# A planned RWKV and MLP kernel: eighth and later weight tiles behind unit 1's diagonal, and a planner with two DMA queues

## The chip, the core and the metric

One core of a Trainium2 chip runs the whole program. Its engines work from instruction queues of their own, each in its written order: TensorE (PE, matmuls, with a row of its own, PEld, for weight loads), VectorE (DVE), ScalarE (ACT), GpSimd (POOL) and SyncE (SP). Semaphores make one engine wait for another. DMAs are requested from SP's queue and from POOL's. The metric is the device time of one execution in microseconds.

## What is computed

An RWKV-like attention runs over 4 batches, 8 heads, 768 steps and 48 channels; two MLPs follow on its 3072 rows of 384 numbers, with 1536 and 2048 hidden columns.

```python
for t in range(S):
    cur = np.einsum('bhd,bhe->bhde', u[None] * kt, vt)
    y[:, :, t] = np.einsum('bhd,bhde->bhe', rt, state + cur)
    state = wt[:, :, :, None] * state + np.einsum('bhd,bhe->bhde', kt, vt)
...
x = (x @ w_a) * (x @ w_b) @ w_out
h = x @ w_in
out = (np.maximum(h, 0) + alpha * np.minimum(h, 0)) @ w_out2
```

## The kernel before, in words

**The attention** is cut into 12 units of 128 steps for half of the batches (`unit`, line 337). A unit has two chunks of 64 steps; in a chunk the step by step sum becomes a triangular matrix `M` (steps by steps) times `v`, plus the state. Pieces of `M` near the diagonal, of 4, 8 or 16 steps (`SUBS`), are summed on DVE from the natural layout `N` (`natural`: products `e`, sums into `A`). The rest of the triangle comes from matmuls on the transposed layout `Tp` (`T` for unit 1), in levels of 4 to 32 steps: `tree` (DVE, line 521) multiplies the decays in, `level` makes the product `psl` on PE, and ACT copies it into `M` (for unit 1 half of it on DVE). The names in the order of a unit: `psl` (levels), `psk` (transposed keys, copied to `kn` by ACT), `psd` (the state's increase), `St` and `Z` (the state and its copies), and at the end `psx` (the unit's result), which ACT casts into `x` with DVE making its remainder. Units 0 and 1 write their triangles to `m` and `M`, and have tiles of their own.

**The diagonal** (`diag`, line 501) goes from `A` to a small buffer `mb` in HBM and comes back into `M` in eight pieces, `d0` to `d3` for two heads: one write and eight loads from SP's queue, each piece a request.

**The first MLP** (`mlp1`, line 778) takes two units at a time, a block, as a right side of 512 columns: 12 steps of 9 `pa`, 9 `pb` and 9 `acc` matmuls. Every factor stands as a high and a low part, so each product is three matmuls. ACT copies `pa` to `a` and casts `g`, DVE multiplies. The attention of the next block runs beside it. After six blocks the second MLP (`hp`, `hb`, `acd`) runs alone.

**The weights** come as 64-bit floats, 128 x 384 to a tile of 0.39 MB (`load_w`, line 271): POOL requests `raw`, ACT takes it apart in three steps (`ws`, `raw`, `ws`), DVE joins (`ws`), ACT casts the high part (`w`), DVE makes the low one (`w`). The tiles of a step of the first MLP are `a`, `b` and `o`. In the kernel before the first tile is requested when a piece of unit 0's diagonal has landed (a one-element copy `tick` on POOL that reads it, `gate`), six tiles can be under way, and the copy ahead of each later request waits for the tile six before it (`behind`, `WL = 6`).

**The order of all this** is made when the program is built, by a list scheduler (`Tasks.run`, line 94). Each task has an engine, a duration that is assumed, a priority (a due time, lower first) and what it reads and writes. The scheduler runs a clock of its own and lets each engine that is free take the first ready task; the order it finds is the written order of each engine's queue. It knows loads as one stream: `DMA_RATE` of 0.33e6 bytes a microsecond, one after the other, and 2.2 us on top. Between 4.5 and 400 us, until the first `pa`, it puts fills on PE (`warm`, matmuls whose result is not used) where PE would have little to do.

## Time and profile before

| | us |
|---|---|
| Three runs, median | 1005.68 |
| Lowest and highest run | 1001.80, 1007.31 |
| The profiled execution | 1007.24 |
| Its span | 1005.5 |

| engine | busy, us | share of the span |
|---|---|---|
| PE | 977.4 | 97% |
| DVE | 727.9 | 72% |
| ACT | 431.3 | 43% |
| POOL | 86.1 | 9% |

The span is from the first to the last instruction; 1.7 us of the execution lie around it. PE's time holds the fills, and matmuls overlap, so 97% is not 97% of its peak. The shares are means over three stages: a start of some 70 us without MLP, a middle to 600 us with attention and first MLP, and the second MLP. In the middle DVE is nearly full, at the end half empty.

### The profile page before, as it was taken

How to read it: one execution, taken by the hardware profiler on the slowest of the kernel's cores; microseconds unless marked ns; L12 is line 12 of the kernel's file. 1: busy time of each engine (PE TensorE's matmuls, PEld its weight loads, DVE VectorE, ACT ScalarE, POOL GpSimd, SP SyncE). 2: the span in 40 equal slices, each digit the busy share in tenths (PEclk: the TensorE clock that was granted, in tenths of full speed). 3: DMA queues.
4: the chain of work that ended last, by engine and by line, in shares of the span. 5: the costliest groups of instructions: out<-in, count | busy, mean ns of one | idle time of the engine just before them, and what ended most of it. 6: DMA issues, size and time to landing. Idle time of an engine off the chain costs nothing.

```text
span 1005.5 us, 21091 instructions
## 1 busy us (share of the span) xinstructions
PE 977.4 (97%) x8800; PEld 822.2 (82%) x8800; DVE 727.9 (72%) x1215; ACT 431.3 (43%) x931; POOL 86.1 (9%) x173
## 2 busy tenths in 40 slices
PE   6989999999999999999999999999999999999998
PEld 3658777878877788778888888898989898999998
DVE  7889989999989979898925668555554646554643
ACT  0696987544535352534438994121211121211111
POOL 1234220100100010000003331000000000000000
PEclk8999999999999999999999999999999999999999
DMA  8795672414333251415026541010100100000000
GB/s 213 189 262 168 179 199 77 135 43 127 85 96 95 68 159 19 129 38 156 17 60 196 181 157 64 1 32 32 32 32 1 32 32 1 32 1 1 32 1 32
DMA packets 78159, 85.61 MB, mean 85 GB/s; under 512 B 55600, under 2 KB 64944, under 8 KB 76784
## 3 DMA queue, kind: packets, MB, share of 16 engines
q1 hardware_dynamic: 70896, 52.81, 19.8%
q0 software_dynamic: 7168, 31.46, 9.7%
q8 instruction: 69, 1.13, 0.5%
q14 instruction: 26, 0.21, 0.1%
HBM read 73.24 MB, written 11.01 MB: 84 GB/s over the span
## 4 chain that ended last, share of the span: by engine, by line
PE 62%; DVE 22%; ACT 7%; DMA 5%; issue 2%; SPq 0%; POOL 0%; DVEq 0%; ACTq 0%; POOLq 0%
PE acd L767 15%; PE hb L767 15%; PE hp L767 10%; PE pa L767 6%; PE pb L767 6%; PE acc L767 6%; DVE e L258 5%; DVE Tp L258 5%; DVE A L482 4%; DMA Tp<-in_rkw_t_dram 3%; DMA N<-in_rkw_n_dram 2%; PE psl L563 2%; DVE N L258 2%; DVE g L258 2%; DVE a L258 2%
## 5 line engine op out<-in xcount | busy, mean ns | idle before, releaser
L767 PE MATMUL acd<-w,g 128*128 128x384 f32 x864 | 192.6, 335 | 0.0
L949 ACT CAST g<-g 128x512 fp32r<-128x512 f32 x96 | 59.6, 621 | 283.0 <-PE hb L767 173.0
L767 PE MATMUL acc<-g,w 128*128 128x512 f32 x648 | 174.4, 398 | 1.1 <-ACT g L829 1.1
L767 PE MATMUL pa<-x,w 128*128 128x512 f32 x648 | 161.2, 393 | 0.7 <-ACT a L818 0.5
L767 PE MATMUL pb<-x,w 128*128 128x512 f32 x648 | 160.0, 391 | 0.7 <-ACT w L317 0.4
L767 PEld LDWEIGHTS acd<-w,g 128*128 128x128 f32 x864 | 154.2, 188 | 1.8
L767 PEld LDWEIGHTS pa<-x,w 128*128 128x128 f32 x648 | 121.0, 189 | 27.8 <-ACT a L818 1.1
L767 PEld LDWEIGHTS pb<-x,w 128*128 128x128 f32 x648 | 120.9, 188 | 27.0 <-ACT w L317 0.9
L767 PEld LDWEIGHTS acc<-g,w 128*128 128x128 f32 x648 | 118.7, 188 | 26.0 <-ACT g L829 1.7
L258 DVE TENSOR_TENSOR g<-g,g 128x512 fp32r<-128x512 f32 x96 | 66.2, 689 | 81.5 <-ACT g L949 80.9
L258 DVE TENSOR_TENSOR Tp<-Tp 112x1024 f32<-112x1024 f32 (+2 forms) x132 | 106.4, 806 | 12.4 <-DMA Tp<-in_rkw_t_dram 7.8
L767 PE MATMUL hp<-x,w 128*128 128x512 f32 x432 | 102.9, 391 | 0.0
L767 PE MATMUL hb<-x,w 128*128 128x512 f32 x432 | 102.0, 389 | 0.0
L767 PEld LDWEIGHTS hb<-x,w 128*128 128x128 f32 x432 | 81.1, 188 | 16.8
L829 ACT CAST g<-a 128x512 fp32r<-128x512 f32 x72 | 44.5, 618 | 117.1 <-DVE a L258 111.5
L767 PEld LDWEIGHTS hp<-x,w 128*128 128x128 f32 x432 | 80.8, 188 | 16.0
L767 PE MATMUL hb<-w,g 128*128 128x384 f32 x288 | 92.5, 335 | 0.0
L482 DVE TENSOR_REDUCE A<-e 128x16 f32<-128x768 f32 (+15 forms) x148 | 85.6, 578 | 1.6
L940 DVE TENSOR_SCALAR g<-hp,al 128x512 f32<-128x512 f32 x48 | 36.0, 750 | 63.0 <-PE hp L767 63.0
L258 DVE TENSOR_TENSOR a<-a,pb 128x512 f32<-128x512 f32 x72 | 49.0, 681 | 22.2 <-PE pb L767 21.5
L818 ACT COPY a<-pa 128x512 f32<-128x512 f32 x72 | 42.0, 583 | 40.9 <-PE pa L767 40.6
L258 DVE TENSOR_TENSOR g<-a,g 128x512 fp32r<-128x512 f32 x72 | 49.3, 685 | 10.7 <-ACT g L829 10.6
(83 smaller groups left out, 1093.0 us busy)
## 6 DMA issues: line engine op xcount, KB each, us to landing
raw<-in_wt_dram POOLq DMA_DIRECT2D x68, 384.0 KB, 4.0
Tp<-in_rkw_t_dram SPq DMA_DIRECT2D x33, 448.0 KB, 5.5
N<-in_rkw_n_dram SPq DMA_DIRECT2D x10, 1152.0 KB, 7.5
x2d<-x POOLq DMA_DIRECT2D x36, 128.0 KB, 2.1
x2r<-x2d SPq DMA_DIRECT2D x36, 128.0 KB, 2.2
out_dram<-o SPq DMA_DIRECT2D x24, 192.0 KB, 1.9
V<-in_v_s_dram SPq DMA_DIRECT2D x11, 384.0 KB, 6.4
Z<-in_v_s_dram SPq DMA_DIRECT2D x44, 96.0 KB, 3.1
```

What stands on the lines that cost most here:

```text
L258: nc.vector.tensor_tensor(out=out, in0=a, in1=b, op=op)
L482: nc.vector.tensor_reduce(out=v[:, :, d:d + (n - 1) * (SUB + 1) + 1:SUB + 1], in_=part(st["e"], 0, n), axis=AX.X, op=ALU.add)
L563: nc.tensor.matmul(out=st["ps"][o0:o0 + ms, cc, q, zc * i:zc * i + zc], lhsT=t[b0:b0 + 48, 1, q0 + q, t0:t0 + ms], rhs=r[b0:b0 + 48, q0 + ...
L767: nc.tensor.matmul(out=out, lhsT=lhsT, rhs=rhs, start=start, stop=stop)
L818: nc.scalar.copy(c["a", f], c["pa"])
L829: nc.scalar.copy(c["g", f][:, 0], c["a", f])
L940: nc.vector.tensor_scalar(out=st["m", f], in0=st["h", f], scalar1=0.0, scalar2=al[:, f:f + 1], op0=ALU.min, op1=ALU.mult)
L949: nc.scalar.copy(st["g", f][:, 0], st["m", f])
```

## The change

**Requests.** The first seven tiles are requested at once behind unit 0's piece. The eighth waits for a piece of unit 1's diagonal (`M1d2`) by a second one-element copy, and each tile from the eighth on for the tile six before it. To make this possible the generators of the tiles are started in another order (`weights`).

**The planner.** `Queues` takes the place of the single stream: the requests of SP and of POOL stand in two lines, whose heads share a rate by the size of their packets; a transfer's cost has a part per packet; one marked `last` (the diagonal's write) goes only when all requests ahead of it are done. Durations of some tasks are set anew (weight steps on ACT, `psl`, `psk`, `psx`, the MLPs' matmuls, some SP requests). And up to 75 us ACT and DVE don't start a task if one that is more urgent by 4 will be ready within 0.5 us (`soon`).

```diff
+class Queues:
+    def __init__(self):
+        self.rings, self.open, self.n, self.t = {}, set(), 0, 0.0
+    def issue(self, key, ring, now, nbytes, packet, kind):
+        rate = 255e3 if kind == "slow" else 400e3
+        cost = nbytes / packet / 16 * (0.009 + packet * 16 / rate)
+        self.open.add(self.n)
+        self.rings.setdefault(ring, []).append(
+            [key, now + (1.0 if ring == "Pool" else 0.4), cost, self.n, kind, min(max(packet, 256), 6144)])
+        self.n += 1
+    def next(self, until):
+        while until > self.t:
+            heads = [q[0] for q in self.rings.values() if q]
+            act = [x for x in heads if x[1] <= self.t + 1e-9 and not (x[4] == "last" and min(self.open) < x[3])]
...
+            share = sum(x[5] for x in act) / (0.87 if len(act) == 1 and act[0][5] > 300 else 1.0)
+            end = min([self.t + min(x[2] / x[5] for x in act) * share, until] + later)
+            for x in act:
+                x[2] -= (end - self.t) * x[5] / share
...
+                    return end + 1.1, x[0]
...
-    DMA_RATE = 0.33e6
-    DMA_LAT = 2.2
...
+        def soon(eng, p, dur):
+            c, at_ = {}, {}
+            for i, end in ends.items():
+                for s in succ[i]:
+                    if t[s][0] == eng and t[s][2] < p - 4.0:
+                        c[s] = c.get(s, 0) + 1
+                        at_[s] = max(at_.get(s, 0.0), end + (self.LAT[t[i][0]] if t[i][0] != eng else self.SAME.get(eng, 0.0)))
+            return any(c[s] == need[s] and at_[s] < now + min(0.5, dur) for s in c)
...
+                        if now < 75.0 and eng in ("ACT", "DVE") and soon(eng, p, t[i][1]):
+                            break
...
         gate = len(prev) == 1
+        second = len(prev) == 7 + 1
         if gate:
             after = list(after) + ["m1/d2"]
-        if len(prev) > WL:
+        if second:
+            after = list(after) + ["M1d2"]
+        if len(prev) > 7:
             behind = prev[-1 - WL]
...
+            if second:
+                nc.gpsimd.tensor_copy(tick, M[96:97, 1, 0, 0, 32:33])
...
-        add("ACT", act(384), pr, sign, r=[raw], w=[ws, raw + "/h"], alloc=("ws", ws))
-        add("ACT", act(384), pr, expo, r=[raw], w=[raw + "/h"])
-        add("ACT", act(384), pr, low, r=[raw, ws], w=[ws])
+        add("ACT", 0.53, pr, sign, r=[raw], w=[ws, raw + "/h"], alloc=("ws", ws))
+        add("ACT", 0.455, pr, expo, r=[raw], w=[raw + "/h"])
+        add("ACT", 0.53, pr, low, r=[raw, ws], w=[ws])
...
-            add("SP", 0.6, p, out_, r=[an], w=[mbn], nbytes=131072)
+            add("SP", 0.6, p, out_, r=[an], w=[mbn], nbytes=131072, packet=1024, kind="last")
...
-            add("PE", 1.2 + 0.22 * nf, p, mms, r=nm(f"{T}/r", bs) + nm(f"{T}/k", bs), w=[ps],
+            add("PE", (1.15 if h == 32 or z == 32 else 1.6 if h == 16 else 1.8) + 0.22 * nf, p, mms, r=nm(f"{T}/r", bs) + nm(f"{T}/k", bs), w=[ps],
...
-    MM = 0.2155
+    MM = 0.228
...
         weights((load_w((nm, f), wt1[f, i], start[0] + (start[1] - start[0]) / F1 * f - wlead + i)
-                 for f in range(F1) for i, nm in enumerate("abo")), WL - 1)
+                 for f in range(F1) for i, nm in enumerate("abo")), WL - 1, 7, 2)
```

**What moves.** First PE's queue from its start to unit 0's last `psl`; `warm` are the fills, the `psl` rows unit 0's levels of 4, 8, 16 and 32 steps. Before:

```order
L1015 MATMUL warm<-idt 128x512 x9
L563 MATMUL psl<-Tp 60x32 x32
L1015 MATMUL warm<-idt 128x512 x3
L563 MATMUL psl<-Tp 56x32 x32
L1015 MATMUL warm<-idt 128x512 x3
L563 MATMUL psl<-Tp 48x32 x32
L1015 MATMUL warm<-idt 128x512 x4
L563 MATMUL psl<-Tp 32x32 x32
```

Now:

```order
L1082 MATMUL warm<-idt 128x512 x11
L630 MATMUL psl<-Tp 60x32 x32
L1082 MATMUL warm<-idt 128x512 x2
L630 MATMUL psl<-Tp 56x32 x32
L1082 MATMUL warm<-idt 128x512 x3
L630 MATMUL psl<-Tp 48x32 x32
L1082 MATMUL warm<-idt 128x512 x5
L630 MATMUL psl<-Tp 32x32 x32
```

The fills lie otherwise: two more ahead of the first level, one fewer behind it, one more ahead of the last. In the same place on DVE's queue (`a` and `A` are the sums of units 0 and 1, `Tp` is unit 0's tree), before:

```order
L258 TENSOR_TENSOR N<-N 128x4x48
L258 TENSOR_TENSOR Tp<-Tp 112x2x512
L258 TENSOR_TENSOR e<-N 128x4x48
L258 TENSOR_TENSOR Tp<-Tp 112x512
L482 TENSOR_REDUCE a_89<-e 128x4
L258 TENSOR_TENSOR Tp<-Tp 112x2x256x2
L258 TENSOR_TENSOR e<-n_91,un 128x768
L258 TENSOR_TENSOR Tp<-Tp 112x256
L258 TENSOR_TENSOR e<-e,n_90 128x768
L258 TENSOR_TENSOR Tp<-Tp 112x2x128x4
```

Now:

```order
L320 TENSOR_TENSOR N<-N 128x4x48
L320 TENSOR_TENSOR e<-N 128x4x48
L549 TENSOR_REDUCE a_89<-e 128x4
L320 TENSOR_TENSOR Tp<-Tp 112x2x512
L320 TENSOR_TENSOR Tp<-Tp 112x512
L320 TENSOR_TENSOR Tp<-Tp 112x2x256x2
L320 TENSOR_TENSOR Tp<-Tp 112x256
L320 TENSOR_TENSOR e<-n_91,un 128x768
L320 TENSOR_TENSOR e<-e,n_90 128x768
L320 TENSOR_TENSOR Tp<-Tp 112x2x128x4
```

The last product and sum of unit 0's diagonal (`e`, `a`) come ahead of the tree's first steps.

The second place is ACT's queue from unit 1's last copy of `psl` to the second cast of its `x`; `raw`, `ws` and `w` are the weight steps. Before:

```order
L669 COPY St_79<-psd_743 112x384
L302 ACTIVATE ws<-raw 128x384
L308 ACTIVATE raw<-raw 128x384
L302 ACTIVATE ws<-raw 128x384
L296 ACTIVATE ws<-raw 128x384
L317 CAST w<-ws 128x384
L308 ACTIVATE raw<-raw 128x384
L718 CAST x<-psx 128x3x128
L317 CAST w<-ws 128x384
L302 ACTIVATE ws<-raw 128x384
L296 ACTIVATE ws<-raw 128x384
L718 CAST x<-psx 128x3x128
```

Now:

```order
L736 COPY St_79<-psd_744 112x384
L384 CAST w<-ws 128x384 x2
L785 CAST x<-psx 128x3x128
L363 ACTIVATE ws<-raw 128x384
L785 CAST x<-psx 128x3x128
```

Nine weight steps stood between the state's copy `St` and the second cast; now there are three.

The third place is PE's queue where the result of unit 5 (`psx`) stands among the last steps of the second block. Before:

```order
L767 MATMUL pb<-x,w 128x512 x9
L767 MATMUL acc_2456<-g_3260,w 128x512
L767 MATMUL acc_2457<-g_3260,w 128x512
L767 MATMUL acc_2458<-g_3260,w 128x512
L767 MATMUL acc_2456<-g_3260,w 128x512
L767 MATMUL acc_2457<-g_3260,w 128x512
L767 MATMUL acc_2458<-g_3260,w 128x512
L767 MATMUL acc_2456<-g_3260,w 128x512
L767 MATMUL acc_2457<-g_3260,w 128x512
L767 MATMUL acc_2458<-g_3260,w 128x512
L708 MATMUL psx<-M,Z 32x64 x64
```

Now:

```order
L834 MATMUL acc_2390<-g_3214,w 128x512
L834 MATMUL acc_2391<-g_3214,w 128x512
L834 MATMUL acc_2392<-g_3214,w 128x512
L834 MATMUL pa<-x,w 128x512 x9
L775 MATMUL psx<-M,Z 32x64 x64
L834 MATMUL acc_2390<-g_3214,w 128x512
L834 MATMUL acc_2391<-g_3214,w 128x512
L834 MATMUL acc_2392<-g_3214,w 128x512
L834 MATMUL pb<-x,w 128x512 x9
L834 MATMUL acc_2390<-g_3255,w 128x512
```

`psx` stood behind the last `pb` of that block and nine `acc` after it; now it stands ahead of that `pb`, right behind the last `pa`.

## Rows read from the trace of the kernel before

**Rows 1.** By stretch: us, busy PE, PEld, DVE, ACT, POOL (instructions), clock, DMA share, GB/s.

```profile
38.00:70.00 32.00, 28.50 (x626) 17.62 (x626) 28.18 (x60) 30.84 (x67) 10.02 (x18) 1.00 0.87 242
70.00:175.00 105.00, 99.85 (x1187) 80.49 (x1187) 96.36 (x167) 86.87 (x200) 23.42 (x43) 1.00 0.58 161
...
600.00:1005.00 405.00, 401.67 (x2037) 365.96 (x2035) 220.62 (x326) 82.06 (x142) 3.21 (x6) 1.00 0.07 23
```

**Rows 2.** The chain that ended last, 0 to 80 us: start, us, what.

```profile
16.76 0.27 DVE e L258
...
19.08 2.85 PE psl L563 x64
21.93 5.13 PE warm L1015 x6
...
28.82 2.77 PE warm L1015 x6
...
47.99 0.47 DVE w L258
...
66.07 0.42 ACT raw L308
66.49 0.54 ACT ws L302
...
70.48 2.36 PE pa L767 x9
72.84 2.06 PE pb L767 x9
74.90 1.88 PE psl L563 x64
```

**Rows 3.** Timeline of ACT, 33 to 39 us; in brackets the idle time before.

```profile
33.26 1.49 ACT L581 COPY m<-psl 16x256 f32<-16x256 f32 x4 [0.32 <-PE psl L563]
...
37.97 1.16 ACT L581 COPY m<-psl 32x512 f32<-32x512 f32 x2 [3.22 <-PE psl L563]
```

**Rows 4.** Busy time by stretch, columns as in rows 1, around the first `psl`.

```profile
20.00:26.00 6.00, 6.00 (x45) 3.64 (x42) 5.32 (x7) 0.00 (x0) 0.00 (x0) 0.50 0.58 143
16.00:34.00 18.00, 14.92 (x206) 9.35 (x207) 13.80 (x19) 4.67 (x26) 3.78 (x7) 0.81 0.72 157
```

**Rows 5.** Timeline, 60 to 66 us: unit 1's copies and `psx`.

```profile
60.83 1.95 DVE L579 COPY M<-psl 8x128 f32<-8x128 f32 x6
...
65.24 2.28 PE L708 MATMUL psx<-M,Z 128*32 128x64 f32 x128 [2.49 <-issue]
```

**Rows 6.** Timeline of SP's queue, 33 to 57 us: requests.

```profile
33.08 9.47 SPq L403 DMA_DIRECT2D Z<-in_v_s_dram  x4
...
48.66 0.33 SPq L507 DMA_DIRECT2D mb<-A  x1
...
52.16 4.98 SPq L514 DMA_DIRECT2D M<-mb  x8
```

**Rows 7.** DMA: unit 0's issues (median us to landing); unit 1's `M` pieces.

```profile
mb<-a SPq DMA_DIRECT2D x1, 128.0 KB, 7.1
m<-mb SPq DMA_DIRECT2D x8, 16.0 KB, 2.0
...
DMA to landing us min/median/max: 2.9/4.4/4.9
```

**Rows 8.** Waits of PE (170 to 520 us) and DVE (70 to 520): total, times, longest.

```profile
PE psl L563 <- DVE Tp L258: 3.5, 4, 2.0
...
DVE a L258 <- PE pb L767: 11.9, 7, 4.1
```

**Rows 9.** Timeline of PE: unit 5's first `psl` and its `psx`.

```profile
218.47 1.21 PE L563 MATMUL psl<-Tp 48*16 48x16 f32 x128 [0.64 <-DVE Tp L258]
...
256.01 1.99 PE L708 MATMUL psx<-M,Z 128*32 128x64 f32 x128
```

More of the change, by code (lines that the diff above doesn't have):

```diff
@@ L30 @@
 BLOCK_OF = {u: j for j, us in enumerate(BLOCKS) for u in us}
+class Queues:
[12 more added lines that the diff above has]
+            act = [x for x in heads if x[1] <= self.t + 1e-9 and not (x[4] == "last" and min(self.open) < x[3])]
+            later = [x[1] for x in heads if x[1] > self.t + 1e-9]
+            if not act:
+                if not later or min(later) > until:
+                    return None
+                self.t = min(later)
+                continue
+            share = sum(x[5] for x in act) / (0.87 if len(act) == 1 and act[0][5] > 300 else 1.0)
+            end = min([self.t + min(x[2] / x[5] for x in act) * share, until] + later)
+            for x in act:
+                x[2] -= (end - self.t) * x[5] / share
+            self.t = end
+            for q in self.rings.values():
+                if q and q[0] in act and q[0][2] <= 1e-6:
+                    x = q.pop(0)
+                    self.open.discard(x[3])
+                    return end + 1.1, x[0]
+        return None
 class Tasks:
@@ L114, in run @@
         busy = {}
[L115 removed]
+        queues = Queues()
         ev = []
@@ L175, in run @@
                             busy[eng] = now + t[i][1]
-                            b = max(dma_free, busy[eng])
-                            dma_free = b + t[i][6] / self.DMA_RATE
-                            end = dma_free + self.DMA_LAT
+                            end = None
+                            queues.issue(i, eng, busy[eng], *self.dma[i])
                         else:
@@ L182, in run @@
                         heapq.heappush(ev, (busy[eng], serial, -1))
-                        serial += 1
-                        heapq.heappush(ev, (end, serial, i))
+                        if end is not None:
+                            serial += 1
+                            heapq.heappush(ev, (end, serial, i))
+                        if end is not None:
+                            ends[i] = end
                         progress = True
@@ L188, in run @@
                 filler()
+            landed = queues.next(ev[0][0] if ev else 1e9)
+            if landed:
+                serial += 1
+                heapq.heappush(ev, (landed[0], serial, landed[1]))
+                continue
             if not ev:
@@ L193, in run @@
                 left -= 1
+                ends.pop(i, None)
                 for h in users.get(i, ()):
@@ L1075, in rwkv_then_moe_kernel, with weights @@
         wlead = 20
-        def weights(gens, n):
+        def weights(gens, n, first=0, lag=0):
             gens = list(gens)
+            done = 0
             for i in range(len(gens) + n):
                 if i < len(gens):
+                    while i == first and done < first - lag:
+                        next(gens[done], None)
+                        done += 1
                     next(gens[i])
-                if i >= n:
-                    next(gens[i - n], None)
+                while i >= first and done <= i - n:
+                    next(gens[done], None)
+                    done += 1
         weights((load_w((nm, f), wt1[f, i], start[0] + (start[1] - start[0]) / F1 * f - wlead + i)
-                 for f in range(F1) for i, nm in enumerate("abo")), WL - 1)
+                 for f in range(F1) for i, nm in enumerate("abo")), WL - 1, 7, 2)
         for j in range(NB):
```

37 lines of the change are left out of this document (20 added, 17 removed).

## The prediction

> **What bounds the kernel now.** I read the busy time by stretches first. From 600 us on TensorE (PE) works 401.67 of 405 us, and from 70 to 175 us 99.85 of 105 [rows 1]: once the MLP matmuls run, PE is the bound, and what goes before them is paid in full. So the start decides, and most of the change is made there. The chain of waits shows what the start ends on: the first `pa` matmul begins at 70.48 us [rows 2], behind the cast of `x` on ACT. From 38 to 70 us ACT is busy 30.84 of 32 us [rows 1]: its queue, in its written order, is what the first `pa` waits for. ACT comes to that stretch from the last two copies of unit 0's triangle, which start at 37.97 us, 3.22 us after the copies before them, when PE gives `psl` [rows 3]. Before that DVE and PE stand for each other: from 16 to 34 us DVE is idle for 18.00 - 13.80 = 4.2 us and PE for 18.00 - 14.92 = 3.1 us, all of it ahead of the first `psl`, and behind that idle time the granted clock is 0.50 from 20 to 26 us [rows 4], its 1.2 GHz level. So the reader should see an early part with gaps, a middle part in which ACT has none, and then PE nearly without gaps to the end.
>
> **The change, part by part.** All is summed against the profiled execution, 1007.24 us, which stands 1.56 us above the median of the three runs, 1005.68 us.
>
> *a. ACT reaches its list earlier.* DVE now does unit 0's last two small steps ahead of the first tree step instead of between its parts (0.27 us each [rows 2]), and puts unit 1's tree behind unit 0's. PE has 11 fills ahead of the first `psl` where it had 9, and then 2, 3 and 5 where it had 3, 3 and 4. A fill is two passes: 2.77/6 = 0.46 us a pass at the full clock, 5.13/6 = 0.855 at the half [rows 2]. The two added in front cover 4 x 0.46 = 1.8 of the 3.1 idle us, and the first `psl` comes 0.6 us earlier, so 0.7 us of idle time is left. If the clock then stays up, the first `psl` takes 1.88 instead of 2.85 us [rows 2], the two fills behind it 1.8 instead of 5.1 for three, and the fill that is added later costs 0.9: -0.6 - 1.0 - 3.3 + 0.9 = -4.0 us until PE gives the last `psl`. DVE, which has 4.2 us of gaps there, can follow. ACT's four copies of the level before started 0.32 us late at 33.26 us and take 1.49 [rows 3]; they can end at 34.4. So the last two start at 34.4 instead of 37.97: **-3.5 us**. If the clock falls as it did, the first `psl` stays at 2.85 us and the four passes cost 3.4: -0.6 - 1.7 + 0.9 = -1.4. The rows show a fall after 3.1 idle us [rows 4], and none after the 2.49 idle us ahead of unit 1's `psx` [rows 5], with 1.00 for all of 38 to 70 us [rows 1]. 0.7 us is nearer to the second; I take -3.5.
>
> The Trainium skill (TensorE: Matmul & The Clock Gate, Part 1: The HAM clock gate) says that the clock goes to its half rate after the engine has been idle and comes back once it has been kept busy. By that rule the part is worth -3.5 us with the gap covered, and -1.4 if the rest of the gap still counts as idle; the trace agrees with its 0.50 behind the long gap.
>
> *b. Fewer weight steps stand ahead of the first `pa`.* Between those two copies and the last cast of unit 1's `x` ACT had 40 weight steps (21 `ws`, 10 `raw`, 9 `w`); now it has 29 (15, 7, 7). All its other steps are the same. In the chain a `ws` step costs 0.54 and a `raw` step 0.42 [rows 2]; I take `w`, of the same size, like `raw`: 6 x 0.54 + 5 x 0.42 = **5.3 us**, gone from a queue that had at most 1.2 us idle [rows 1].
>
> *c. What is late next.* ACT's steps behind the weights need unit 1's diagonal. Its way out is asked for at 48.66 us and its pieces leave from 52.16 us on, for 4.98 us [rows 6]; a piece lands 4.4 us after its request (4.9 at most), where unit 0's, with no weight tile under way, took 2.0 [rows 7]. In the change the write goes out when DVE has the last sum. Ahead of it DVE loses 4.2 us of gaps, three weight steps of 0.47 [rows 2], and three small steps (0.7): 48.66 - 6.3 = 42.4 us. SP, in order, is held by the `Z` loads until 33.08 + 9.47 = 42.55 [rows 6], and the seventh tile, now asked for at once, is 0.39 MB more on the same engines, at 242 GB/s [rows 1] 1.6 us. Write at 43.5, pieces from 47 (3.5 us, as now) to 52, landed at 54; with 4.9 us a piece, 57. Today DVE copies beside them at 60.83 us, and `psx` starts 65.24 - 60.83 = 4.4 us later [rows 5]. So `psx` starts at 58.4 or at 61, 6.8 or 4.2 us earlier. From `psx` to `pa` it is 5.24 us now, with nine weight steps on ACT ahead of the second cast; three are left, which ACT does beside `psx`, but PE has two fills behind `psx` (2.0 + 4 x 0.46 = 3.8 us): another -1.4.
>
> ACT's own sum, a and b, is -8.8; PE's fills behind `psx` end 1 us after ACT's cast, so -7.8. The diagonal's is -8.2, or -5.6. The later counts: **the first `pa` comes 7.8 us earlier, near 62.7 us**, bounds -5.6 and -8.8.
>
> *d. What comes back.* The 11 ACT steps and 4 DVE weight steps aren't gone, they come after 63 us. ACT has 18 us free from 70 to 175 us, DVE 8.6 [rows 1]. Four DVE steps are 4 x 0.47 = 1.9 us: nothing if they fall into DVE's gaps, all if DVE has none. DVE is nearer to full: **+1.0 us**.
>
> *e. Eighth tile behind the diagonal.* The copy that gates it holds POOL's queue, and with it all later tiles, until a piece lands, near 52 us. The eighth tile belongs to the third `pb`; five groups of nine (2.06 us each [rows 2]), two `psl` and six `acc` go before it: some 15 us after the first `pa`, at 78 us. Asked for at 52, with 4.4 us to land and 3 on ACT and DVE, it is there at 60. Cost 0; without that cover it is what the pieces are late beyond 70 us.
>
> *f. New durations in the planner.* They move pieces of the attention units on PE by up to 6 us between 70 and 500 us; the second MLP is issued as before. PE's waits for the tree are 3.5 us there in four places [rows 8]. I take 0: -3.5 is what could be won, and the loss is the third rival.
>
> Sum: -7.8 + 1.0 = -6.8 us, 1000.4 us for an execution like the profiled one and **998.9 us** against the median.
>
> **The rivals.**
>
> 1. *DVE is the bound behind the start.* From 70 to 175 us it is busy 96.36 of 105 us [rows 1]. Then PE gains what DVE gains: part a, -3.5, less 1.9 for the steps put off, is -1.6; up to -5 if DVE waits less. For it: PE's waits for `Tp` [rows 8]. Against: DVE itself waits 11.9 us for PE's `pb` [rows 8], so it is often ahead. About 1002.5 us.
>
> 2. *The diagonal lands no earlier.* Seven tiles and the loads of `v` are under way when its write is asked for. Unit 0's write, behind its loads, took 7.1 us [rows 7]; then pieces leave from 51 us and with 4.9 us each land at 61, as now, and ACT waits for them where it did weights. 0 to -1.4: about 1005 us. Against: by 48 us most of what is under way has landed in any case.
>
> 3. *PE stands for unit 5's `psx`.* In the new order that unit's first `psl` comes 27 MLP matmuls later and its `psx` 21 earlier; at 2.06/9 = 0.229 us [rows 2] 6.2 and 4.8 us. Today they start 256.01 - 218.47 = 37.5 us apart [rows 9], then 26.5. If the steps between need all 37.5 us, PE stands 11 us with the MLP queued behind, and the time is 999 + 11 = 1010 us, slower. The sign turns where they need over 33.3 us (6.8 more than 26.5). Against: DVE and ACT do other work in those 37.5 us, the MLP's above all, and PE does not stand idle at that `psx` today.
>
> **How the numbers follow.** A measurement of this kernel can tell about 0.5%, 5.0 us, from no change, so faster is under 1000.7. The forecast, with a start of -5.6 to -8.8, 0 to 1.9 back and up to 3.5 fewer waits, spans 993.4 to 1002; chance 0.60, a small part of it above 1000.7. Rival 1 has 0.22, now and then under 1000.7; rival 2 0.09; rival 3 0.09, most of it over 1010.7 or near it, the rest made up by the start. Faster 0.56, same 0.37, slower 0.07. The range, 993 to 1006 us, leaves out rival 3 and the ends.
>
> **What would show it.** Right: the full clock from 20 to 26 us; the diagonal's write near 43 us, its pieces landed at 54; the first `pa` at 61 to 65 us; the second MLP's first `hp` some 7 us earlier than now. Wrong: a first `pa` that is early but PE waits, for `Tp`, `kn` or `Z`, that have grown by several us between 170 and 440 us (rivals 1 and 3), or a first `pa` near 69 us with ACT waiting for the pieces (rival 2).

## The result and the profile after

The change made the kernel slower: 1012.18 us (median of 8 runs, 1008.15 to 1015.72) against 1005.65 us (8 runs of the kernel before beside them), ratio 1.0064, 95% interval 1.0043 to 1.0085. 998.9 us was forecast. The profiled execution took 1011.55 us with a span of 1009.8 us, 4.3 us more than the span of before.

By stretch, the kernel after (us, busy PE, PEld, DVE, ACT, POOL with instructions, granted clock, DMA share, GB/s); the second, third and last rows answer to [rows 1], the first to [rows 4]:

```profile
20.00:26.00 6.00, 6.00 (x74) 3.17 (x72) 5.97 (x9) 0.61 (x4) 0.00 (x0) 1.00 0.21 39
38.00:70.00 32.00, 28.39 (x631) 19.30 (x630) 25.51 (x54) 27.28 (x62) 7.19 (x15) 1.00 0.85 219
70.00:175.00 105.00, 94.57 (x1154) 74.22 (x1153) 91.65 (x161) 86.07 (x197) 31.86 (x44) 0.98 0.58 159
...
600.00:1005.00 405.00, 405.00 (x2052) 368.88 (x2051) 221.90 (x330) 86.33 (x150) 4.74 (x9) 1.00 0.07 22
```

The clock no longer falls to 0.50 between 20 and 26 us. But from 70 to 175 us PE is busy 5.3 us less than before (94.57 against 99.85), and it pays for that: at the second MLP, where PE is full in both, the kernel after is 4.3 us late.

**The start came as forecast.** The timelines of the kernel after (start, us, engine, line, operation, in brackets the idle time before and what ended it), of ACT, of SP's queue and of PE; they answer to [rows 3], [rows 6] and the `psx` of [rows 5]:

```profile
33.42 1.17 ACT L648 COPY m<-psl 32x512 f32<-32x512 f32 x2 [1.00 <-PE psl L630]
```

```profile
42.21 1.36 SPq L574 DMA_DIRECT2D mb<-A  x1
...
45.79 6.34 SPq L581 DMA_DIRECT2D M<-mb  x8
...
82.50 0.35 SPq L455 DMA_DIRECT2D N<-in_rkw_n_dram  x1
83.23 0.33 SPq L574 DMA_DIRECT2D mb<-A  x1
91.67 4.29 SPq L581 DMA_DIRECT2D M<-mb  x8
```

```profile
58.88 0.65 PE L775 MATMUL psx<-M,Z 128*32 128x64 f32 x32
61.13 1.60 PE L775 MATMUL psx<-M,Z 128*32 128x64 f32 x96 [1.59 <-ACT Z L726]
62.66 1.98 PE L1082 MATMUL warm<-idt 128*128 128x512 f32 x4
64.65 2.34 PE L834 MATMUL pa<-x,w 128*128 128x512 f32 x9
```

Unit 0's last copies start 4.55 us earlier, unit 1's diagonal leaves 6.45 us earlier, the first `pa` starts 5.83 us earlier (70.48 before).

**Then it is lost inside block 0.** The `pb` of step 4 still starts 5.4 us earlier than before (94.9 against 100.3 us), the `pb` of step 5 3.5 us later (112.1 against 108.6). PE's timeline there, kernel after:

```profile
100.46 1.20 PE L630 MATMUL psl<-Tp 48*32 48x32 f32 x64 [2.63 <-ACT M L648]
...
109.81 0.68 PE L700 MATMUL psd<-V,kn 64*48 64x48 f32 x32 [0.21 <-ACT kn L681]
112.09 3.79 PE L834 MATMUL pb<-x,w 128*128 128x512 f32 x9 [1.60 <-ACT w L384]
...
123.73 1.67 PE L834 MATMUL pb<-x,w 128*128 128x512 f32 x6 [0.41 <-DVE w L320]
126.40 1.84 PE L630 MATMUL psl<-Tp 48*56 48x32 f32 x64 [1.00 <-PE pb L834]
```

and ACT's, with the whole stage's busy time under it:

```profile
97.40 0.48 ACT L384 CAST w<-ws 128x384 fp32r<-128x384 f32 x1
97.79 0.84 ACT L648 COPY M<-psl 4x64 f32<-4x64 f32 x6
98.99 2.30 ACT L648 COPY M<-psl 20x64 f32<-20x64 f32 x14 [0.36 <-DMA M<-mb]
...
101.96 3.61 ACT L648 COPY M<-psl 8x128 f32<-8x128 f32 x10
105.60 1.04 ACT L666 COPY M<-Tp 48x1024 f32<-48x1024 f32 x1
...
111.54 0.49 ACT L384 CAST w<-ws 128x384 fp32r<-128x384 f32 x1
```

```profile
96.00:130.00 34.00, 27.95 (x408) 21.48 (x407) 31.58 (x60) 32.35 (x84) 14.24 (x13) 0.95 0.66 180
```

and the same stretch in the kernel before:

```profile
96.00:130.00 34.00, 32.21 (x385) 25.76 (x385) 32.14 (x60) 30.92 (x82) 7.31 (x16) 1.00 0.68 200
```

The reader should see one knot. Unit 2's copies of `M` stand on ACT ahead of the weight tile that step 5 needs (tile 16, counting from 0). ACT comes to them at 97.79 us and does no weight step from there until 108.8 us. So PE first stands 2.63 us at a level that waits for those copies, then 1.60 us for the tile, cast at 111.54 us (98.5 before). The diagonal is late as well, since its write stands behind the 1.15 MB load of `N`, 8.4 us from the write (83.23) to the first piece (91.67); but ACT stood only 0.36 us for its pieces. Behind PE's waits the granted clock is at its lower level, 0.50, from 112.7 to 116.1 us, and nine `pb` matmuls take 3.79 us where the first `pa` took 2.34.

The later blocks lost hardly anything: from the last `pb` of block 0 to the first `hp` the kernel before takes 432.6 us and the kernel after 433.9.

### The profile page after: what moved, and what is told of

It is laid out like the page before. It is cut to its first block, busy times and chain, and to the rows that moved or that the text cites. A ratio compares the mean times of both kernels' runs of the same rounds, so it can differ in the third digit from the quotient of the medians.

```text
span 1009.8 us, 21082 instructions
## 1 busy us (share of the span) xinstructions
PE 979.4 (97%) x8802; PEld 822.0 (81%) x8802; DVE 727.9 (72%) x1215; ACT 432.8 (43%) x931; POOL 92.0 (9%) x173
## 4 chain that ended last, share of the span: by engine, by line
PE 63%; DVE 20%; DMA 7%; ACT 5%; issue 3%; SPq 1%; POOL 0%; DVEq 0%; ACTq 0%; POOLq 0%
PE acd L834 15%; PE hb L834 15%; PE hp L834 10%; PE pb L834 7%; PE acc L834 6%; PE pa L834 6%; DVE e L320 4%; DVE Tp L320 4%; DVE A L549 4%; DMA N<-in_rkw_n_dram 3%; PE psl L630 2%; DVE a L320 2%; DVE N L320 2%; DMA Tp<-in_rkw_t_dram 2%; DVE g L320 2%
## 5 line engine op out<-in xcount | busy, mean ns | idle before, releaser
L834 PE MATMUL pb<-x,w 128*128 128x512 f32 x648 | 164.5, 398 | 4.0 <-ACT w L384 1.6
```

Of the source, the lines that this page charges most:

```text
L834: nc.tensor.matmul(out=out, lhsT=lhsT, rhs=rhs, start=start, stop=stop)
```

## The experiments

All runs in one table; times are of the profiled execution, "last `pb`" is the start of the last `pb` of that block, ratios are to the kernel before, with 95% intervals. Kernels with the same order up to 160 us agree in their last `pb` of block 0 within 3.4 us (the change, e9, e12 and e13: 170.1, 168.4, 169.4, 171.1; e4 and e7: 162.5, 165.3; e5, e10 and e15: 158.1, 154.8, 154.7) and in their first `pa` within 2.8 us (e2 and e16: 67.4, 64.6), so smaller differences there aren't read. One execution stands behind each row's places. The 109 executions of the kernel before that were taken beside the experiments lie between 1000.59 us (mean granted clock 0.998) and 1012.74 us (0.992), so a few us at the first `hp` can be the execution's own: e5's profiled one took 1009.23 us with a median of 1005.30, e13's 1007.77 with 1004.14. For the whole time the medians and ratios count.

| | first `pa` | last `pb`, block 0 | last `pb`, block 4 | first `hp` | median | ratio |
|---|---|---|---|---|---|---|
| before | 70.5 | 167.1 | 524.9 | 599.7 | 1005.65 | 1 |
| the change | 64.6 | 170.1 | 529.2 | 604.0 | 1012.18 | 1.0064 (1.0043 to 1.0085) |
| e1 requests only | 69.7 | 174.0 | 538.3 | 613.1 | 1017.57 | 1.0113 (1.0079 to 1.0147) |
| e2 planner only | 67.4 | 166.9 | 526.6 | 601.4 | 1010.66 | 1.0048 (1.0025 to 1.0071) |
| e3 old durations | 67.8 | 169.8 | 521.0 | 595.8 | 1004.15 | 0.9996 (0.9977 to 1.0015) |
| e4 old DMA model | 69.2 | 162.5 | 528.9 | 603.7 | 1012.18 | 1.0070 (1.0045 to 1.0095) |
| e5 casts first | 65.1 | 158.1 | 526.6 | 601.4 | 1005.30 | 1.0001 (0.9983 to 1.0019) |
| e6 next `N` later | 64.5 | 169.7 | 532.6 | 607.4 | 1013.83 | 1.0076 (1.0049 to 1.0103) |
| e7 two-stage models | 70.6 | 165.3 | 516.5 | 591.4 | 997.37 | 0.9914 (0.9888 to 0.9941) |
| e8 one duration by 0.6% | 67.3 | 172.6 | 525.4 | 600.2 | 1007.94 | 1.0027 (1.0006 to 1.0048) |
| e9 late old durations | 63.5 | 168.4 | 518.2 | 593.0 | 1002.13 | 0.9964 (0.9945 to 0.9983) |
| e10 both mended | 66.7 | 154.8 | 516.8 | 591.7 | 998.44 | 0.9923 (0.9896 to 0.9951) |
| e11 three mended | 70.5 | 160.7 | 515.3 | 590.1 | 997.60 | 0.9912 (0.9884 to 0.9939) |
| e12 late MLP duration | 65.2 | 169.4 | 529.4 | 603.4 | 1013.15 | 1.0072 (1.0047 to 1.0098) |
| e13 pieces planned later | 65.4 | 171.1 | 525.5 | 600.3 | 1004.14 | 0.9982 (0.9958 to 1.0006) |
| e14 casts 25, late old | 65.0 | 152.1 | 514.0 | 588.8 | 995.54 | 0.9893 (0.9861 to 0.9924) |
| e15 casts, pieces later | 66.8 | 154.7 | 519.8 | 593.2 | 1003.82 | 0.9979 (0.9956 to 1.0001) |
| e16 old requests, late old | 64.6 | 168.5 | 522.0 | 597.1 | 1004.23 | 0.9968 (0.9947 to 0.9990) |

**e1, the requests alone** (to the kernel before):

```diff
+        if second:
+            after = list(after) + ["M1d2"]
-        if len(prev) > WL:
+        if len(prev) > 7:
...
-                 for f in range(F1) for i, nm in enumerate("abo")), WL - 1)
+                 for f in range(F1) for i, nm in enumerate("abo")), WL - 1, 7, 2)
```

> The kernel before with the change's requests alone: seven tiles asked for at once, the eighth behind a piece of unit 1's diagonal, two fewer weight steps in hand than before at the start, and the old planner with its one-stream DMA model and old durations. In the planned order the 32x32 levels of unit 2 stand behind 141 MLP matmuls of block 0, where before had 132 and the change has 117. Theory A (the loss comes from the planner's new order in block 0: unit 2's 32x32 levels and its diagonal's copies go ahead of a weight tile whose cast then is late, while its pieces land late): the start gains as in the change, first pa near 64 to 65 us, the gain of some 5.8 us stays through steps 5 and 6 of block 0, 1000 us, ratio 0.995 to the kernel before. Theory B (the loss comes from the requests: two tiles fewer in hand, so the casts run dry at step 5 whatever the order): the tiles of steps 5 and 6 are cast 10 us late as in the change, first hp near 604 us, 1010 to 1013 us.

The worst of all, 1017.57 us, above B's range too, and against theory A: with the old planner the first `pa` is hardly earlier, and tile 10 is cast at 92.3 us (75.6 before). The profiled execution, the longest of its six, has seven drops of the clock. That is B's direction; but this kernel has an order of its own, so it can't say whether the requests or that order made it.

**e2, the planner alone** (the change with the old requests: e1's diff undone).

> The change with the old requests (six tiles at once, every later one behind the one six before it, no second gate), and the new planner: queue model, new durations, the rule that waits for a task about to come ready. Unit 2's 32x32 levels stand behind 117 MLP matmuls as in the change. Theory A (the new order is the loss): unit 1's diagonal lands as late as before, so nothing is gained at the start, and block 0 still stalls near its steps 5 and 6: 1008 to 1018 us, ratio 1.005 to 1.012. Theory B (the requests are the loss): the tiles come as early as before, no stall at step 5, 1003 to 1006 us, ratio 0.997 to 1.000.

Theory A's side: 1.0048, and step 5's `pb` at 112.0 us as in the change. But the diagonal left at 42.6 us all the same, and the first `pa` came 3.1 us earlier than before: a good half of the start's gain comes without the new requests (e16, with the same order there, has nearly all of it).

**e3, old durations** (the change, with):

```diff
-    MM = 0.228
+    MM = 0.2155
...
-        add("ACT", 0.53, pr, sign, r=[raw], w=[ws, raw + "/h"], alloc=("ws", ws))
+        add("ACT", act(384), pr, sign, r=[raw], w=[ws, raw + "/h"], alloc=("ws", ws))
...
-            add("PE", 1.0, p, mms, w=[ps], alloc=(pool, ps), work=2048,
+            add("PE", 1.56, p, mms, w=[ps], alloc=(pool, ps), work=2048,
...
```

> The change with the old durations in the planner (matmul 0.2155, levels 1.2, weight casts by the old formula, and so on); the queue model, the waiting rule and the requests stay. Unit 2's 32x32 levels stand behind 150 MLP matmuls. Theory A (the place of unit 2's levels and copies in the order decides): start as in the change, first pa 64 to 65 us, no wait of a level for the copies of M in block 0, the gain of 4 to 6 us reaches the end: 1000 to 1002 us. Theory B (the requests decide): 1010 to 1013 us, the tile of step 5 late again.

1004.15 us, but not for theory A's reason: no level waits for the copies of `M` and step 5's `pb` is early (104.8 us), but PE then stands 1.65 us for the tile of step 6's `pb` (119.7 us), and block 0 ends as late as in the change (169.8 us). The 8 us are won behind it, 351.2 us from block 0's last `pb` to block 4's where the change takes 359.1. That was new: a second cost, which the comparison of the change with the kernel before had hidden, since both pay it.

**e4, old DMA model** (the change, with the queue model taken out):

```diff
+        dma_free = 0.0
...
-                            end = None
-                            queues.issue(i, eng, busy[eng], *self.dma[i])
+                            b = max(dma_free, busy[eng])
+                            dma_free = b + t[i][6] / 0.33e6
+                            end = dma_free + 2.2
```

> The change with the old one-stream DMA model in the planner (0.33 MB per us behind one another and 2.2 us); new durations, waiting rule and requests stay. Unit 2's 32x32 levels stand behind 114 MLP matmuls, as early as in the change. Theory A (the place of unit 2's levels in the order decides, and the new durations put it there, not the queue model): stall at steps 5 and 6 as in the change, 1009 to 1014 us. Theory C (the queue model makes the bad order): the stall goes, 1000 to 1003 us. Theory B (requests): 1010 to 1013 us.

The time is A's, the mechanism isn't: block 0 ends 7.6 us earlier than in the change, without the stall at step 5, although unit 2's levels stand as early; then 366.4 us to block 4's last `pb`. So the queue model makes block 0's bad order, theory C's part, and something else makes the later blocks slow.

**e5, casts first** (the change, with the casts of block 0's tiles more urgent):

```diff
         yield
+        if key[0] in "abo" and 9 <= 3 * key[1] + "abo".index(key[0]) < 36:
+            pr = pr - 35
         add("ACT", 0.53, pr, sign, r=[raw], w=[ws, raw + "/h"], alloc=("ws", ws))
```

> The change with one thing put back to front in the planner's priorities: the casts of block 0's weight tiles from the tenth on are 35 more urgent, so ACT and DVE do them ahead of units 2's and 3's copies of M and Z. Requests, models and durations are the change's. Unit 2's 32x32 levels stand behind 132 MLP matmuls, its psx behind 222 (the change: 117 and 153). Theory A (block 0 loses the start's 5.8 us because ACT does unit 2's M copies ahead of the tile that step 5 needs, as the planner's new costs and unchanged priorities order it): tile 16 is cast before 103 us (the change 111.5), step 5's pb starts near 104 us (112.1), no half clock near 113 us, block 0's last pb 158 to 164 us (170.0); what is left at the first hp depends on blocks 1 to 4, where units 2 and 3 come later: 998 to 1010 us. Theory B (the requests, two tiles fewer in hand, starve the casts): tile 16 is still cast after 108 us since it was asked for late, block 0 ends at 168 to 171 us, 1009 to 1014 us.

ACT's and PE's timelines of this kernel:

```profile
93.08 0.51 ACT L384 CAST w<-ws 128x384 fp32r<-128x384 f32 x1
...
100.85 0.64 ACT L363 ACTIVATE ws<-raw 128x384 f16<-128x384 f32 x1 [4.88 <-DMA raw<-in_wt_dram]
...
103.10 1.04 ACT L650 COPY M<-psl 4x64 f32<-4x64 f32 x8
```

```profile
105.93 1.92 PE L632 MATMUL psl<-Tp 48*32 48x32 f32 x64 [4.44 <-ACT M L650]
...
109.23 3.04 PE L836 MATMUL pb<-x,w 128*128 128x512 f32 x9
```

With the change's own requests tile 16 is cast at 93.08 us and block 0 ends 12.0 us earlier: theory A for block 0, and against B. Two misses: step 5's `pb` still waits (109.2 us), now behind a level whose copies ACT makes after 4.88 idle us for a tile (here the requests do hold it), and a lower clock follows, 0.50 from 104 us on for 6.8 us. And 368.5 us to block 4's last `pb`, 9.4 more than in the change, give most of it back: 1.0001. Some of the 9.4 is this execution's, which stands 3.9 us above its median.

**e6, unit 3's `N` behind unit 2's diagonal**:

```diff
-            add("SP", 0.6 if u != 1 else 1.8, p0 if u > 1 else p0 + -1, ld_n, r=after_diag,
+            add("SP", 0.6 if u != 1 else 1.8, p0 if u > 1 else p0 + -1, ld_n, r=after_diag if u != 3 else diags[1],
```

> The change with unit 3's load of N (1.15 MB) behind unit 2's diagonal pieces, so that unit 2's mb write has no large transfer right ahead of it. Theory A2 (the stall of step 5 begins with the late diagonal: mb written behind N, 8.4 us to its pieces in the change, 4.9 us before): write to pieces 5 to 6 us, the wait of 2.6 us of psl for ACT's copies of M is under 1 us, step 5's pb 3 us earlier, block 0's end 2 to 3 us earlier, 1007 to 1010 us. Rival (ACT's order decides, not the transfer): the order puts unit 2's 32x32 levels still earlier (behind 105 MLP matmuls, 117 in the change), tile 16 is cast as late, unit 3 comes later by its own N: 1011 to 1016 us.

SP's queue and PE of this kernel:

```profile
82.89 0.35 SPq L574 DMA_DIRECT2D mb<-A  x1
84.86 4.11 SPq L581 DMA_DIRECT2D M<-mb  x8
89.02 0.44 SPq L455 DMA_DIRECT2D N<-in_rkw_n_dram  x1
```

```profile
116.41 2.94 PE L834 MATMUL acc<-g,w 128*128 128x512 f32 x9 [3.23 <-ACT g L896]
...
125.97 2.33 PE L834 MATMUL acc<-g,w 128*128 128x512 f32 x9 [1.50 <-ACT g L896]
```

The write's way is shown: 2.0 us to the first piece without `N` ahead, 8.4 with it. And it is not the cause of the loss: the wait for the copies of `M` is gone, tile 16 is still cast only at 109.1 us, PE waits for `g` instead, 1013.83 us. The rival's outcome: ACT's order decides.

**e7, two stages of models**:

```diff
+LATER = 160.0
...
+                            if now < LATER:
+                                b = max(dma_free, busy[eng])
+                                dma_free = b + t[i][6] / 0.33e6
+                                end = dma_free + 2.2
+                            else:
+                                end = None
+                                queues.issue(i, eng, busy[eng], *self.dma[i])
...
+                        if now >= LATER:
+                            t[i][1] = self.alt.get(i, t[i][1])
...
```

(`alt` holds the old durations.)

> The change's requests, with the planner's models switched at 160 us of planned time (about the end of block 0): before that the old one-stream DMA model and the new durations (as in the run with the old DMA model, whose block 0 ended 4.7 us earlier than the kernel before), after it the queue model and the old durations (as in the run with the old durations, whose blocks 1 to 4 took 6.6 us less than those of the kernel before). If the two stages are separate and each result belongs to its model: block 0 the same as in the run with the old DMA model (last pb 162 to 163 us), blocks 1 to 4 some 350 us from there to the first hp less 6: first hp 589 to 592 us, 994 to 998 us, ratio 0.989 to 0.993. If what follows is a matter of how the list happens to fall (any small change of it moves blocks 1 to 4 by several us either way): first hp 593 to 604 us, 998 to 1010 us.

997.37 us, as expected of two separate costs (block 0 ended at 165.3 us, 2.3 over its own range): 351.2 us from block 0's last `pb` to block 4's, the figure of e3.

**e8, one duration moved by 0.6%** (`MM = 0.2267` for `0.228`, nothing else).

> The change with one duration of the planner moved by less than one per cent: MLP matmuls planned at 0.2267 us and not 0.228. Nothing else. If the loss is the effect of the requests or of the models as such, this changes nothing that matters: 1010 to 1014 us, first hp 602 to 606 us, block 0's end 168 to 171 us. If the planner's list is so sensitive that a sub-per-cent duration moves it, the time moves by more than 4 us either way, 1002 to 1008 or over 1016 us, and single results of model changes can't be read as the effect of that model.

4.2 us less than the change, at the edge of what was called sensitive. Step 5's `pb` stays late (114.4 us) and block 0 ends at 172.6; the later blocks gain 6. So block 0's loss stands against a small push, while a few us in the later blocks can come from the way the list falls, and single results of that size there are weak evidence.

**e9, old durations from 160 us on** (e7 with the queue model kept all through).

> The change up to 160 us of planned time (block 0 in the change's own order, start and requests included); from there on the old durations, with the queue model kept. Theory D (the new durations cost blocks 1 to 4 some 3 us each: with a longer MLP matmul the planner puts psx behind 3 to 22 fewer MLP matmuls, so that it meets the diagonal's pieces before they land, and PE waits): block 0 ends as in the change (its last pb at 170 to 173 us), psx of units 4 to 11 waits for no piece of M, blocks 2 to 4 take 87.5 us each (the change: 90.3, 90.9, 90.7), first hp 593 to 597 us, 999 to 1004 us. Rival (how the list happens to fall): blocks 2 to 4 take 89 to 92 us again in at least two of the three, first hp 600 to 606 us, 1006 to 1014 us.

By stretch, this kernel (columns as above):

```profile
260.00:345.00 85.00, 84.96 (x1096) 69.36 (x1097) 82.01 (x143) 40.77 (x94) 2.15 (x4) 1.00 0.39 101
345.00:435.00 90.00, 90.00 (x1227) 73.62 (x1227) 83.89 (x147) 40.73 (x94) 3.21 (x6) 1.00 0.33 91
435.00:525.00 90.00, 90.00 (x970) 73.86 (x959) 66.21 (x121) 41.57 (x86) 5.67 (x13) 1.00 0.28 77
```

and in its place in the change:

```profile
260.00:525.00 265.00, 259.28 (x3231) 211.17 (x3230) 229.76 (x403) 116.65 (x261) 10.43 (x21) 0.99 0.31 85
```

As theory D has it: 1002.13 us, 10 less than the change, with block 0 as it was. PE has 0.04 idle us from 260 to 525 us where the change has 5.72. Blocks 3 and 4 take 87.6 us each; block 2 takes 91.1, not 87.5, since unit 5's `psx` stands behind block 1's last `pb` here. Where PE stood longest in the change, its timeline:

```profile
297.02 0.27 PE L775 MATMUL psx<-M,Z 128*32 128x64 f32 x2 [0.94 <-DMA M<-mb]
...
384.33 0.30 PE L775 MATMUL psx<-M,Z 128*32 128x64 f32 x2 [1.10 <-issue]
...
429.24 0.27 PE L775 MATMUL psx<-M,Z 128*32 128x64 f32 x2 [0.70 <-DMA M<-mb]
...
491.95 3.15 PE L834 MATMUL pb<-x,w 128*128 128x512 f32 x7 [1.55 <-issue]
```

Of the 5.72 us only 2.0 are waits for pieces, with a second, short one behind each of the waits at 297 and 429 us. The 1.10 us at unit 8's `psx` are none: its last piece had landed at 381.0 us. Nor are the 1.55 us in the middle of nine `pb`, which have no releaser in the trace; the granted clock is 0.50 for 3.4 us there (from 491.6 us). So theory D's mechanism, `psx` ahead of its pieces, is seen, but it is a third of PE's idle time in these blocks.

**e10, e9 with e5's casts.**

> The kernel of the run before this one in the list, with the casts of block 0's tiles from the tenth on 35 more urgent as in the run with the casts first. Theories A and D together (block 0 loses by ACT's order, blocks 1 to 4 by the place of psx): block 0's last pb ends near 160 us as there, blocks 2 to 4 take 87.5 us, first hp 584 to 590 us, 990 to 996 us, ratio 0.985 to 0.990. If units 2 and 3, which come later for it, hold block 1 back: first hp 592 to 597 us, 998 to 1004 us.

998.44 us. Block 0 ends at 154.8 us, even earlier than in e5, but block 1 and 2 then take 91.1 and 95.1 us: the time is that of the expectation's second case, in which units 2 and 3 come later and hold block 1 back. Why block 2 is slow as well isn't shown.

**e11, e7 with e5's casts.**

> The two-stage models (old DMA model up to 160 us of planned time, queue model and old durations after it) with block 0's casts 35 more urgent. Theories A and D together: block 0's last pb near 158 to 162 us, blocks 2 to 4 at 87.5 us, first hp 584 to 590 us, 990 to 996 us. Rival (the queue model matters in block 0 for unit 1's start too, so the old DMA model loses the first 3 to 6 us): block 0's last pb 163 to 167 us, first hp 589 to 594 us, 995 to 1000 us.

997.60 us, within the rival's 995 to 1000: the old DMA model loses the start (first `pa` 70.5 us). Block 0's last `pb`, 160.7 us, is where theories A and D have it and not the rival; but blocks 2 and 3 take 88.6 and 90.8 us, not 87.5. No better than e7.

**e12, the MLP duration alone put back** (from 160 us on; `psx`, levels and the rest stay new).

> The change with one duration alone put back from 160 us of planned time on: the MLP matmuls of 512 columns (and those of the second stage) at the old, shorter durations; levels, psx, transposes and requests keep the new ones. psx of units 8 to 11 then stands behind 39 to 66 more MLP matmuls than in the change. Theory D (the place of psx behind the MLP matmuls is what costs, and the longer MLP duration moved it): no wait of psx for pieces of M, blocks 2 to 4 at 87.5 us, first hp 593 to 597 us, 999 to 1004 us. Rival (the durations of levels and psx cost): psx waits as in the change, blocks of 89 to 92 us, 1006 to 1014 us.

1013.15 us, against theory D as it was put: `psx` hardly waits for pieces (0.33 us at unit 7's), and blocks 2 to 4 take 93.1, 92.3 and 91.3 us all the same. So not "a longer MLP duration is bad". PE stands elsewhere:

```profile
265.42 0.66 PE L637 MATMUL psl<-Tp 48*16 48x16 f32 x61 [1.26 <-issue]
...
310.49 1.16 PE L637 MATMUL psl<-Tp 48*16 48x16 f32 x106 [1.75 <-issue]
...
358.78 0.33 PE L637 MATMUL psl<-Tp 48*16 48x16 f32 x22 [1.66 <-issue]
```

Here `psx` stands late, and a unit's first level comes close behind the `psx` of the unit before. PE stops in the midst of that level's 128 matmuls, and the trace gives no releaser. These places have something in common: in PE's list (weight loads, matmuls and semaphore instructions) they are numbers 6594, 7617 and 8898, and the change's 1.10 and 1.55 us stand at 9666 and 12225, all a multiple of 256 apart, within one. In the 18 traces together PE has 44 idle times over 0.6 us without a releaser behind 40 us, and 42 of them lie on this grid. So they go with the place in PE's list and not with a piece or a tile; what PE stands for there, and why only at some of these places, no run tests.

**e13, the pieces believed 3 us later** (all new durations kept):

```diff
-                heapq.heappush(ev, (landed[0], serial, landed[1]))
+                heapq.heappush(ev, (landed[0] + (3.0 if now > 160.0 and self.dma[landed[1]][1] == 64 else 0.0), serial, landed[1]))
```

> The change with all its durations; only, from 160 us of planned time on, the planner believes that a diagonal's pieces land 3 us later. psx of units 4 to 9 moves behind 9 to 18 more MLP matmuls (459 to 474, 618 to 630, 765 to 783, 915 to 927, 1068 to 1077, 1239 to 1251), the last two by 3 and 6. Theory D' (what costs is that psx, on PE's queue in order, stands ahead of the landing of its pieces): psx waits for pieces under 0.5 us in each unit from 4 to 9, blocks 2 and 3 take 87.5 to 88.5 us (the change: 90.3 and 90.9), first hp 595 to 599 us, 1001 to 1006 us. Rival (the longer durations cost by something else in the order, such as levels that wait for the tree): blocks of 90 us and more, first hp over 601 us, 1008 to 1014 us.

No `psx` waits for a piece any more, and 1004.14 us, 8 less than the change, with every new duration in place. Blocks 3 and 4 take 87.6 and 88.0 us (90.9 and 90.7 in the change). So the new durations needn't cost. That `psx` ahead of its pieces is all of the cost isn't shown, since the change's 1.10 and 1.55 us without a releaser are gone too. The first `hp` missed its range by 1.3 us in an execution 3.6 us above its median, and block 2 missed its own (93.9 us, 87.5 to 88.5 expected), with one wait and a clock at 0.50 for 3.4 us behind it:

```profile
326.64 1.72 PE L700 MATMUL psd<-V,kn 64*48 64x48 f32 x64 [2.12 <-ACT kn L681]
```

**e14, e10 with casts 25 more urgent and not 35.**

> As the run with both mended, with casts 25 more urgent and not 35, so that units 2 and 3 come earlier (unit 2's psx behind 189 MLP matmuls and not 222, unit 3's behind 324 and not 318). Theories A and D add up where units 2 and 3 don't hold block 1 back: block 0's last pb near 157 to 162 us, block 1 to 246 to 248 us, blocks 2 to 4 at 87.5 us, first hp 584 to 588 us, 990 to 994 us. If they don't: first hp 590 to 594 us, 996 to 1000 us, as the three best so far.

By stretch:

```profile
70.00:175.00 105.00, 101.09 (x1194) 81.35 (x1193) 98.32 (x171) 89.65 (x203) 40.97 (x50) 1.00 0.58 166
96.00:130.00 34.00, 33.34 (x384) 26.57 (x384) 32.69 (x61) 33.45 (x87) 15.35 (x22) 1.00 0.67 208
...
260.00:525.00 265.00, 262.48 (x3258) 214.59 (x3257) 230.22 (x406) 121.25 (x271) 11.24 (x25) 1.00 0.32 90
```

995.54 us, ratio 0.9893 (0.9861 to 0.9924): the best, it beats both kernels. It keeps the start (first `pa` at 65.0 us), PE works 101.09 of 105 us in block 0's stretch (94.57 in the change), and the clock stays at its full level over the whole span. From 96 to 130 us ACT is fuller than in the change (33.45 us against 32.35), and PE works 33.34 of 34 us: it is the order on ACT and not its free time that decides there. The median is 1.5 us over its range. Block 0 ended earlier than expected (152.1 us) and block 1 where it was expected (245.9); the miss is in blocks 2 and 3, 89.3 and 91.2 us where 87.5 was expected, with waits of 1.04 and 1.11 us for the tree.

**e15, the change with e5's casts and e13's later pieces.**

> The change with all its durations and both orders mended by what is late: casts of block 0 35 more urgent, and the pieces believed 3 us later from 160 us on. Theories A and D' together: block 0's last pb near 157 to 161 us, psx without waits for pieces, first hp 587 to 593 us, 993 to 999 us. If the place of psx was not the cost: blocks 2 to 4 as in the run with the casts first (90.4, 93.7, 93.2), first hp 598 to 602 us, 1003 to 1007 us.

The first `hp` is at 593.2 us, at the edge; the median of 1003.82 is 4.8 us over the range, its profiled execution 1002.41. So e13's mending carries over only in part: no `psx` waits for a piece, and still blocks 2 to 4 take 93.5, 88.1 and 92.3 us, where e5 has 90.4, 93.8 and 93.2. `psx` ahead of its pieces isn't all that costs there.

**e16, e9 with the old requests.**

> The kernel of the run with the late old durations (the change up to 160 us of planned time, old durations from there on), with the old requests. Theory A with the requests worth nothing or a little less by the end: first pa near 67.4 us (3 us later than with the new requests), block 0's last pb 166 to 168 us (168.4 with the new ones), first hp 590 to 594 us, 999 to 1003 us, ratio 0.994 to 0.998: the same as with the new requests. If the new requests help the whole by their earlier start: 1004 us or more. Theory B (the new requests are the loss): tile 16 cast before 105 us, block 0's last pb before 164 us, 995 to 998 us.

0.9968 with the old requests, 0.9964 with the new: no difference against the kernel before. The median itself, 1004.23 us, lies 1.2 us over the expected range, the first `hp` (597.1) 3.1 us; in microseconds this is the case "1004 us or more", but the kernel before took 1.3 us more beside it than beside e9. Tile 16 is asked for at 77.7 us (84.6 in e9) and still cast at 109.4 (110.0). Theory B is out where the planner is the new one. The first `pa` came at 64.6 us, not 67.4: that, too, is nearly the same without the new requests.

## Why the prediction was wrong, point by point

- *Part a, ACT's list earlier, clock up: right.* -4.55 us where -3.5 was taken, with a granted clock of 1.00 from 20 to 26 us.
- *Part b, fewer weight steps ahead: right in kind.* ACT was no longer full from 38 to 70 us (27.28 us busy, 30.84 before), and waited where it had worked.
- *Part c, the diagonal: right, the size off by 2 us.* Its write left at 42.21 (43.5 forecast), the pieces from 45.79 (47), `psx` started at 58.88 (58.4 or 61). `psx` to `pa` took 5.8 us and not 3.8, since `psx` stopped 1.59 us for ACT's copies of `Z`. First `pa` -5.8: the lower bound of 5.6 to 8.8, not -7.8.
- *Part e, the gate of the eighth tile: right, cost 0* (e16).
- *Part d, what comes back: the step that failed.* +1.0 us was taken, 0 to 1.9, because "ACT has 18 us free from 70 to 175 us". Come back did all of the 5.8 us and some 3.0 more by the end of block 0; with 1.3 us more in the later blocks that makes -5.8 + 8.8 + 1.3 = +4.3 us at the first `hp`. The 18 us are a mean: from 96 to 130 us ACT was busy 30.92 of 34 us in the kernel before and 32.35 after. And free time wasn't the measure: e14 keeps ACT fuller there and loses next to nothing, so what costs is which step ACT does first. PE's idle time from 64.65 to 175 us is 10.43 us (0.12 to 96, 6.05 to 130, 4.26 to 175 us); before, 6.39 from 64 to 175 (111.00 - 104.61), the wait ahead of the first `pa` among it. The drop of the clock adds some 1.5 us (3.79 against 2.34 for nine matmuls). The order of ACT's queue is fixed when the program is built and could have been read before; the prediction looked only at the start and at unit 5.
- *Part f, the planner's models: 0 was taken, wrong twice over.* The queue model makes block 0's order bad: between first `pa` and last `pb` the change takes 105.5 us, the kernel before 96.6, e4 and e7 93.3 and 94.7, e5 93.0, e14 87.1. In blocks 1 to 4 the queue model wins 6.6 us with the old durations (e3: 351.2 us, before 357.8), and the new durations take it back (359.1). The prediction's part f looked for a cost in waits for the tree (3.5 us); PE's stops in the change from 260 us on are mostly others (e9).
- *The rivals.* Rival 3's mechanism came true at other places: PE stood for a `psx` that its order had put ahead of its diagonal, not 11 us at unit 5 (its `psx` at 254.56 us didn't wait), but 0.94 and 0.70 us at units 6 and 9, 2.0 us with the short waits behind them; the 1.10 us at unit 8's came after its pieces had landed. It can't carry the loss. Rival 2 fell, the diagonal was early. Rival 1, DVE as the bound, fell as well: DVE was busy less than before (91.65 of 105 us), and e14 has 98.32. A rival that was missing: *ACT's order in block 0 as the bound*.

Theory A is shown for block 0 by e5 and e16 (and e14): the same requests with casts first win 12 us there, the old requests with the same order win nothing. For blocks 1 to 4, e9 shows that the new durations used from 160 us on cost some 10 us as this order fell, and e13 that later landings in the plan win most of that back. Theory D', that `psx` ahead of its pieces is the cost, is shown only for the 2.0 us of such waits; the rest of the cost, PE's stops without a releaser among it, stays open, and e8, e12 and e15 show that a gain of a few us there is not safe. Two things weren't taken apart: why the requests alone (e1) cost 1.1% under the old planner, and the rule `soon`, which every run but e1 keeps, so that its part in block 0's order is unknown.

## What to carry to other kernels

A gain at the start is worth only what the next stage can keep: read the engines' free time at the place where the moved work lands (3.08 of 34 us on ACT before, where the mean over the stage promised 18 of 105) and not over the whole stage, and follow every engine's order there, not only that of the bound. When a scheduler gets other numbers, even truer ones (0.228 us for a matmul that takes 0.229), its priorities, which are left as they were, can turn wrong: with the queue model it held the casts back behind copies that were more urgent on paper, and with the longer matmul times it put two `psx` ahead of their pieces. Where in-order queues meet uncertain landings, slack can stand in the plan as such (e13); here it did no better than old durations that happened to leave it (e9).

## What was not expected of the hardware

- A write of 0.13 MB right behind a request of 1.15 MB on the same queue: 8.4 us to the first load that reads it back, 2.0 without that request ahead (e6). The Trainium skill (DMA: Bandwidth & Descriptors, Queues, rings and completion order) says that each DMA engine consumes its descriptors in ring order; the two runs agree with it.
- After short waits of PE (2.63, 0.21 and 1.60 us within 12 us) the granted clock was 0.50, its 1.2 GHz level, for 3.4 us. Nine `pb` matmuls took 3.79 us, so a wait can cost about as much again in clock.
- PE stops of 0.6 to 2.9 us without a releaser lie at places in its list that are a multiple of 256 instructions apart (42 of 44 in all traces, e12). They show only at some of these places, in e12 where `psx` and a level of 128 matmuls each come close behind one another.
